# A fused attention and gated feed-forward kernel: how its last chunk is summed, transposed and stored, and where a small product of denominators stands

## The chip, the cores and the metric

The kernel runs on one core of a Trainium2 chip. The time is device microseconds of one execution. The five runs before the change gave 297.88, 298.35, 299.22, 299.48 and 301.63 us; their median is 299.22 us. A profile was taken of one further execution, and its trace has a time for every instruction of every engine.

## The reference

Everything is fp32.

```python
# attention: q, k, v are (4 batches, 4 heads, 1088 positions, 32)
a = einsum('rd,bhsd->bhsr', S1, x);  b = einsum('rd,bhsd->bhsr', S2, x)   # r = 8
phi(x) = (a outer b), 64 features
kv  = einsum('bhsf,bhsd->bhfd', phi(k), v);   z = sum(phi(k), axis=2)
num = einsum('bhsf,bhfd->bhsd', phi(q), kv)
den = einsum('bhsf,bhf->bhs', phi(q), z)[..., None] + 1e-06
x   = (num / den), laid out as (4352 tokens, 128)
# feed-forward: w_gate, w_val (128, 1536), w_out (1536, 128)
out = (1 / (1 + exp(-(x @ w_gate))) * (x @ w_val)) @ w_out
```

## The kernel before

The tokens of all four batches stand in one SBUF tensor `xT`, model dimension on partitions. Within a batch its columns are ordered so that 32 successive columns are 32 tokens that lie 34 apart in the output. The feed-forward part goes over `tok_chk`: chunks 0 to 7 of 512 tokens and chunk 8 of 256.

For a chunk, `w1` (lines 456 to 521) makes one wave at a time: the gate and value products of 128 hidden units for 512 tokens (in chunk 8: of 256 hidden units for 256 tokens, so six waves instead of twelve). ScalarE takes the sigmoid (line 479), VectorE the product `g` (line 501, run one slot later by `glu`). Then `g` is multiplied with `w_out`, in one of two ways:

- Chunks 1 to 7 use seven products in place of eight (`w2_a` and `w2_b`, matmuls at line 338, called `prod`), with sums of `g` made on GpSimd. When the last product of a chunk has been issued, five pieces of VectorE work are left: three steps of sums (line 410), a 64-partition transpose (line 445), and a second transpose followed by the chunk's stores. They are put into the list `moe["late"]`, and `slot` takes one of them per wave.
- Chunks 0 and 8 use `w2` (lines 362 to 386, matmuls at line 373, called `moeout`): `w_out` is stationary, `g` moves, and the result has the output features on partitions. A VectorE transpose (line 383) turns it in 32 x 32 blocks, and `store` writes it in four DMAs of one 32-feature group each, in runs of 32 numbers (128 bytes). For chunk 8 two of the four go out on ScalarE's queue, the others on SyncE's (SP). Chunks that cross a batch have eight.

In the trace one fp32 matmul of the program appears as two matmul instructions, each with a weight load. A matmul of 64 output rows uses half of the array's columns; two of them that write different halves run side by side.

The order of work is written by hand. `slot(group, waves)` first runs a piece of the attention part, then for each wave: `glu`, one item of `late`, every item of `todo` that has come due, and the next `w1`. `todo` holds the `w_out` products, with lags of 2 to 4 waves behind their `g`; when there are no more waves, the rest is issued one after the other. So chunk 7's five late pieces fall into the waves of chunk 8.

For the batches 1 to 3, `parts(b)` (line 1174) makes a batch's output of the attention. `den_j` (lines 930 to 943) multiplies into the PSUM tile `two`, and VectorE makes `pd` of it. `dn(b, n)` (line 972) issues the numerators of one half of the batch (`nps`, line 1000): n = 1 into the PSUM tile `wave`, n = 0 into the tile `two`, which is free again when `pd` has been made. `den_i` (line 946) multiplies `pd` with a mask into the spare columns of the `wave` tile (`nps`, line 949). `turn_den` transposes that and takes reciprocals on VectorE (line 961 on), and `divide1` and `divide0` write the quotients into `xT`.

PSUM tiles come from pools: `psm` has two buffers of the tile `wave`, `ps2` one of the tile `two`, each two banks wide. An instruction waits for semaphores of other engines; TensorE, VectorE and ScalarE each take their instructions in the order in which they were issued.

Of the kernel before, what the change touches and what calls it, by code (L numbers as in the profile page):

```python
# [8 lines left out]
F32 = mybir.dt.float32  # L9
# [7 lines left out]
P = 128  # L17
# [3 lines left out]
def kernel(  # L21
# [12 lines left out]
    nc = tc.nc  # L34

    B, H, S, D = q.shape
    R = S1.shape[0]
    F = R * R
    NTOK, DM = out.shape
    DFF = moe_w_gate.shape[1]  # L40
    NJ = DFF // P
    assert DM == H * D == P and D == 32 and R == 8 and S % 32 == 0

    T = S // 32

# [3 lines left out]
    TCH = 512  # L49
    tok_chk = [(o, min(TCH, NTOK - o)) for o in range(0, NTOK, TCH)]  # L50
# [3 lines left out]
    sbA = ctx.enter_context(tc.tile_pool(name="sbA", bufs=2))  # L54
# [7 lines left out]
    pso = ctx.enter_context(tc.tile_pool(name="pso", bufs=1, space=bass.MemoryType.PSUM))  # L62
    ps2 = ctx.enter_context(tc.tile_pool(name="ps2", bufs=1, space=bass.MemoryType.PSUM))
# [81 lines left out]
    w_sb = const.tile([P, 3, NJ, P], F32, tag="w_sb", name="w_sb")  # L145
# [133 lines left out]
    for c in range(2):  # L279
        rows = slice(64 * c, 64 * c + 64)  # L280
        nc.vector.tensor_reduce(
            out=m_col[rows, c],
            in_=ident[rows].rearrange("p (k j) -> p j k", j=R),
# [3 lines left out]
    for t, x in (  # L287
# [5 lines left out]
        out=e_sum,  # L293
        in_=bass.AP(
            tensor=e_row.tensor,
            offset=e_row.offset,
            ap=[list(e_row.ap[0]), [0, 2], [1, R], [0, R]],
        ),
# [43 lines left out]
    def store(ci, rows):  # L342
        t0, tw = tok_chk[ci]
        c = t0
        while c < t0 + tw:
            b, r = divmod(c, S)
            n = min(t0 + tw - c, S - r) // 32
            u = (c - t0) // 32
            for g4 in range(4):

                eng = nc.scalar if ci == len(tok_chk) - 1 and g4 % 2 else nc.sync
                eng.dma_start(
                    out=bass.AP(
                        tensor=out.tensor,
                        offset=out.offset + (b * S + r // 32) * DM + 32 * g4,
                        ap=[[T * DM, 32], [DM, n], [1, 32]],
                    ),
                    in_=rows(g4)[:, u : u + n, :],
                )
            c += n * 32  # L360

    def w2(ci, j0, jn, g):
        t0, tw = tok_chk[ci]
        if j0 == 0:
            moe["sum"] = ci
            if ci == 0:
                moe["acc"] = pso.tile([P, TCH], F32, tag="acc0", name="moeout")
            else:
                moe["acc"] = ps2.tile([P, 2, TCH], F32, tag="two", name="moeout")[:, 0]
        for jj in range(jn):  # L370
            j = j0 + jj
            for d in (slice(0, P),) if ci == 0 else (slice(0, 64), slice(64, P)):
                nc.tensor.matmul(  # L373
                    out=moe["acc"][d, :tw],
                    lhsT=w_sb[:, 2, j, d],
                    rhs=g[:, jj, :tw],
                    start=(j == 0),
                    stop=(j == NJ - 1),
                )
        if j0 + jn == NJ:  # L380
            o_sb = sbA.tile([P, 2, TCH // 32, 32], F32, tag="o_sb", name="o_sb")[:, 0]
            nt = tw // 32
            nc.vector.transpose(
                out=o_sb[:, :nt, :].rearrange("p t d -> p (t d)"), in_=moe["acc"][:, :tw]
            )
            store(ci, lambda g4: o_sb[32 * g4 : 32 * g4 + 32])


    fst = {}
# [66 lines left out]
    def w1():  # L456

        ci = moe["ci"]
        t0, tw = tok_chk[ci]
        jn = TCH // tw  # L460
        j0 = moe["w"] * jn
        wv = psm.tile([P, 2, TCH], F32, tag="wave", name="wave")

        tp = tw // 2 if ci == 0 and j0 == 0 else tw
        turn = (moe["w"] // 2) % 2
        for o in range(0, tw, tp):
            for which in range(2):
                for jj in range(jn):
                    for c in (0,) if ci == 0 else (1 - turn, turn):
                        d = slice(0, P) if ci == 0 else slice(64 * c, 64 * c + 64)  # L470
                        nc.tensor.matmul(  # L471
                            out=wv[d, which, jj * tw + o : jj * tw + o + tp],
                            lhsT=w_sb[:, which, j0 + jj, d],
                            rhs=xT[:, t0 + o : t0 + o + tp],
                            start=True,
                            stop=True,
                        )
        sg = sbG.tile([P, TCH], F32, tag="sg", name="sg")
        nc.scalar.activation(out=sg, in_=wv[:, 0], func=ACTF.Sigmoid)  # L479
        if ci == 0:  # L480
            if j0 == 1:
                narrow_01(2, 3)
            if 0 < j0 < NJ - 2:
                narrow_w(j0 + 1, 3)
            narrow_w(j0 + 2, 1)
            narrow_w(j0 + 2, 2)
            if j0 < 3:
                narrow_w(j0 + 3, 0)
            if j0 > 1:
                narrow_w(j0 + 4, 0)  # L490
            if j0 == NJ - 3:
                weight_sums(0, NJ // 4)
        if ci == 1 and j0 == 1:
            weight_sums(NJ // 4, NJ // 2)
        if moe["w"] % 2 == 0:
            moe["g"] = sbG.tile([P, 2, TCH], F32, tag="g", name="g")
        pair, odd, n = moe["g"], moe["w"] % 2, moe["n"]

        def glu():
            g = pair[:, odd]  # L500
            nc.vector.tensor_tensor(out=g, in0=wv[:, 1], in1=sg, op=MUL)  # L501
            todo = moe["todo"]
            if not fast(ci):
                lag = 3 if ci else 2
                part = (ci, j0, jn, g.rearrange("p (j t) -> p j t", j=jn))
                todo.append((n + lag, lambda: w2(*part)))
                return
            if not odd:
                moe["t"] = raw.tile([P, 4, HALF], F32, tag="w_in", name="tsum")
            token_sums(pair, moe["t"], odd)  # L510
            if odd:
                part = (ci, j0 // 2, pair, moe["t"])
                todo.append((n + 3, lambda: w2_a(*part)))
                todo.append((n + 4, lambda: w2_b(*part)))

        moe["gate"] = glu
        moe["w"] += 1
        moe["n"] += 1
        if j0 + jn == NJ:
            moe["ci"] += 1  # L520
            moe["w"] = 0
# [6 lines left out]
    def slot(group, waves):  # L528

        if group is not None:  # L530
            group()
        todo = moe["todo"]
        for _ in range(waves):
            more = moe["ci"] < len(tok_chk)
            if more and sum(tok_chk[moe["ci"]]) > moe["ready"]:
                break
            glu()
            if moe["late"]:
                moe["late"].pop(0)()
            while todo and todo[0][0] <= moe["n"]:  # L540
                todo.pop(0)[1]()
            if more:
                w1()
            elif not todo:
                break
            else:
                todo.pop(0)[1]()
# [398 lines left out]
    def den_i(b, t):  # L946
        dps = t[:, 0, W1 : W1 + WD]
        for h in range(H):
            nc.tensor.matmul(
                out=dps[32 * h : 32 * h + 32],  # L950
                lhsT=mask["head"][:, h % 2, :],
                rhs=PD[b][:, h // 2, :],
                start=True,
                stop=True,
            )
        return dps

    def turn_den(b, dps):
        nt, over = WD // 32, (W1 - WD) // 32
        dT = sbA.tile([P, nt, 32], F32, tag="dTi", name="dTi", bufs=1)  # L960
        nc.vector.transpose(out=dT.rearrange("p t c -> p (t c)"), in_=dps)
        RC[b] = sbA.tile([P, 2, W1 // 32, 2], F32, tag="rci", name="rci")
        for t0, t1, u0, k in ((0, nt, 0, 0), (nt, W1 // 32, nt - over, 4)):
            nc.vector.tensor_scalar_add(
                RC[b][:, :, t0:t1],
                dT[:, u0 : u0 + t1 - t0, k : k + 4].rearrange("p t (n c) -> p n t c", n=2),
                1e-6,
            )
        nc.vector.reciprocal(out=RC[b], in_=RC[b])
# [88 lines left out]
    else:  # L1058
        nc.vector.tensor_copy(
            out=s4[:, 1:],  # L1060
# [8 lines left out]
        out=st_[:, : 2 * R],  # L1069
        lhsT=s4.rearrange("p g d -> p (g d)"),  # L1070
# [103 lines left out]
    def parts(b):  # L1174
        den_j(b)
        glu()
        t = psm.tile([P, 2, 512], F32, tag="wave", name="nps")
        divide1 = dn(b, 1, t=t)
        divide0 = dn(b, 0)
        dps = den_i(b, t)  # L1180
        turn_den(b, dps)
        divide1()
        divide0()

# [101 lines left out]
```

## Time and profile before

| | us |
|---|---|
| median of five runs | 299.22 |
| lowest and highest run | 297.88, 301.63 |
| the profiled execution's own time | 301.79 |
| its span, from the first to the last instruction | 300.0 |
| TensorE busy with matmuls | 289.6 |
| VectorE busy | 187.1 |
| GpSimd busy | 161.4 |
| ScalarE busy | 88.8 |

The profile is of one core. PE stands for TensorE's matmuls and PEld for its weight loads, DVE for VectorE, ACT for ScalarE, POOL for GpSimd, SP for SyncE; SPq and ACTq are the queues on which SP and ScalarE issue DMAs. L373 is line 373 of the kernel. A row of the timeline gives the start, the duration (of all that it merges), the engine, the line, the operation, output and input with partitions x elements, the count, and in brackets the idle time before it with what ended it. A row of the waits gives the waiting instruction, what it waited for, the sum in us and how often. Matmul records overlap, since matmuls are pipelined.

### The profile page before, as it was taken

To read this page: it belongs to the slowest core of one execution; us is meant where nothing else is said; L and a number is where in the kernel's file an instruction comes from. 1 tells how busy PE (TensorE), PEld (TensorE's weight loads), DVE (VectorE), ACT (ScalarE), POOL (GpSimd) and SP (SyncE) were. 2 spreads that over 40 slices of the span, in tenths; PEclk is the share of its full clock that TensorE was granted. 3 is DMA by queue.
4 is the path that set the end of the run, shared out by engine and by line. 5 is a ranking of instruction groups with operands and counts; after the bars stand their busy time and mean duration, and the time that the engine had idled before them with its cause. 6 is when DMAs were issued, how large, how long until landed. Compare 5 with 4: busy or idle time off the path is not lost.

```text
span 300.0 us, 5678 instructions
## 1 busy us (share of the span) xinstructions
PE 289.6 (97%) x2224; PEld 154.9 (52%) x2224; DVE 187.1 (62%) x317; ACT 88.8 (30%) x164; POOL 161.4 (54%) x221
## 2 busy tenths in 40 slices
PE   8899999997999999999999999999999999999993
PEld 3444432353455456554455555554565655555892
DVE  6997789974725766677656695667436423643353
ACT  3556523222023222331223222422232222322320
POOL 2465553992364657645456498554455555565200
PEclk9999999999799999999999999999999999999998
DMA  7994340774700058426000475102000200020003
GB/s 225 356 327 101 101 139 13 163 154 103 237 0 0 11 132 165 129 76 177 9 0 2 124 176 111 26 0 37 1 2 0 35 2 0 0 37 0 2 0 52
DMA packets 29689, 24.21 MB, mean 81 GB/s; under 512 B 19616, under 2 KB 24864, under 8 KB 29664
## 3 DMA queue, kind: packets, MB, share of 16 engines
q1 hardware_dynamic: 28752, 23.10, 30.3%
q10 hardware_dynamic: 912, 0.77, 1.0%
q8 instruction: 17, 0.28, 0.4%
q14 instruction: 8, 0.07, 0.1%
HBM read 20.60 MB, written 3.26 MB: 80 GB/s over the span
## 4 chain that ended last, share of the span: by engine, by line
PE 76%; DMA 13%; DVE 4%; POOL 2%; SPq 2%; issue 1%; ACT 1%; POOLq 0%; ACTq 0%
PE wave L471 49%; PE prod L338 20%; DMA bq<-dq 5%; PE moeout L373 3%; DMA w_in<-in_moe_w_out_dram 2%; POOL head L118 2%; DMA w_in<-in_moe_w_gate_dram 2%; DMA v<-in_v_dram 2%; DVE w_sb L127 1%; PE nps L1000 1%; DMA kq<-in_k_dram 1%; DVE head L109 1%; SPq L758 1%; DMA dq<-cq 1%; PE kvz L806 1%
## 5 line engine op out<-in xcount | busy, mean ns | idle before, releaser
L471 PE MATMUL wave<-xT,w_sb 128*64 128x512 f32 (+3 forms) x820 | 211.5, 566 | 0.1
L501 DVE TENSOR_TENSOR g<-wave,sg 128x512 f32<-128x512 f32 x102 | 70.0, 687 | 86.8 <-ACT sg L479 85.4
L471 PEld LDWEIGHTS wave<-xT,w_sb 128*64 128x64 f32 (+1 forms) x820 | 85.5, 140 | 64.7 <-issue 49.3
L479 ACT ACTIVATE sg<-wave 128x512 f32<-128x512 f32 x102 | 61.0, 598 | 184.3 <-PE wave L471 183.1
L328 POOL TENSOR_TENSOR tsum<-g 128x256 f32<-128x256 f32 x84 | 68.0, 812 | 26.1 <-DVE g L501 25.9
L328 POOL TENSOR_TENSOR tsum<-g,tsum 128x256 f32<-128x256 f32 x42 | 34.2, 814 | 66.6 <-DVE g L501 66.1
L338 PE MATMUL prod<-tsum,ws 128*64 128x256 f32 x252 | 64.2, 384 | 0.0
L338 PEld LDWEIGHTS prod<-tsum,ws 128*64 128x64 f32 x252 | 31.8, 138 | 15.8 <-issue 10.9
L338 PE MATMUL prod<-g,w_sb 128*64 128x256 f32 x168 | 34.8, 382 | 0.0
L328 POOL TENSOR_TENSOR tsum<-tsum,g 128x256 f32<-128x256 f32 x42 | 32.8, 780 | 3.3
L338 PE MATMUL prod<-tsum,w_sb 128*64 128x256 f32 x84 | 25.9, 390 | 0.0
L338 PEld LDWEIGHTS prod<-g,w_sb 128*64 128x64 f32 x168 | 15.9, 136 | 17.7 <-issue 15.3
L338 PE MATMUL prod<-g,ws 128*64 128x256 f32 x84 | 25.0, 379 | 0.0
L118 POOL TENSOR_TENSOR head<-head,tail 128x384 int32<-128x384 int32 (+2 forms) x14 | 13.4, 954 | 18.2 <-DVE head L109 12.9
L373 PE MATMUL moeout<-g,w_sb 128*64 128x256 f32 (+1 forms) x72 | 18.7, 456 | 0.3 <-DVE w_sb L127 0.3
L338 PEld LDWEIGHTS prod<-g,ws 128*64 128x64 f32 x84 | 11.5, 137 | 3.3
L338 PEld LDWEIGHTS prod<-tsum,w_sb 128*64 128x64 f32 x84 | 10.9, 138 | 4.5 <-issue 4.0
L786 DVE TENSOR_TENSOR qp<-qp,bq 128x1152 f32<-128x1152 f32 (+1 forms) x7 | 9.6, 1374 | 5.1 <-DMA bq<-dq 3.7
L373 PEld LDWEIGHTS moeout<-g,w_sb 128*64 128x64 f32 (+1 forms) x72 | 8.8, 154 | 7.0 <-issue 2.8
L666 DVE TENSOR_TENSOR kp<-kab 128x1152 f32<-128x1152 f32 (+2 forms) x10 | 10.7, 1082 | 0.0
L445 DVE STREAM_TRANSPOSE o_sb<-res 64x512 f32<-64x512 f32 x14 | 9.6, 688 | 0.0
L410 DVE TENSOR_TENSOR res<-prod,other 64x512 f32<-64x512 f32 (+1 forms) x14 | 7.6, 544 | 2.8 <-ACT other L404 2.8
(111 smaller groups left out, 185.1 us busy)
## 6 DMA issues: line engine op xcount, KB each, us to landing
qp<-dq SPq DMA_DIRECT2D x7, 576.0 KB, 10.4
bq<-dq SPq DMA_DIRECT2D x14, 288.0 KB
kq<-in_k_dram SPq DMA_DIRECT2D x3, 544.0 KB, 4.1
kq<-in_q_dram SPq DMA_DIRECT2D x3, 544.0 KB
w_in<-in_moe_w_out_dram SPq DMA_DIRECT2D x6, 256.0 KB
w_in<-in_moe_w_gate_dram SPq DMA_DIRECT2D x5, 256.0 KB
w_in<-in_moe_w_val_dram SPq DMA_DIRECT2D x5, 256.0 KB, 6.4
out_dram<-o_sb SPq DMA_DIRECT2D x20, 64.0 KB, 2.3
```

The source lines that it names most:

```text
L109: nc.vector.scalar_tensor_tensor(out=head, in0=cap, scalar=-0x40000000, in1=head, op0=ALU.bitwise_and, op1=ALU.bitwise_or)
L118: nc.gpsimd.tensor_tensor(out=head, in0=head, in1=tail, op=ALU.add)
L328: nc.gpsimd.tensor_tensor(out=t[:, u], in0=in0, in1=in1, op=ALU.subtract)
L338: nc.tensor.matmul(out=out, lhsT=lhsT, rhs=rhs, start=start, stop=stop, skip_group_check=True)
L373: nc.tensor.matmul(out=moe["acc"][d, :tw], lhsT=w_sb[:, 2, j, d], rhs=g[:, jj, :tw], start=(j == 0), stop=(j == NJ - 1),)
L410: nc.vector.tensor_tensor(out=out, in0=in0, in1=in1, op=op)
L445: nc.vector.transpose(out=o_sb[:64, d].rearrange("p t x -> p (t x)"), in_=r[:, 1 + 2 * d : 3 + 2 * d].rearrange("p u x -> p (u x)"),)
L471: nc.tensor.matmul(out=wv[d, which, jj * tw + o : jj * tw + o + tp], lhsT=w_sb[:, which, j0 + jj, d], rhs=xT[:, t0 + o : t0 + o + tp], sta ...
L479: nc.scalar.activation(out=sg, in_=wv[:, 0], func=ACTF.Sigmoid)
L501: nc.vector.tensor_tensor(out=g, in0=wv[:, 1], in1=sg, op=MUL)
L666: eng.tensor_tensor(out=KP[b][:, pi, j0:j1].rearrange("p j m (i l) -> p (j m) i l", i=R), in0=bass.AP(tensor=a0.tensor, offset=a0.offset, ...
L786: nc.vector.tensor_tensor(out=q0, in0=q0, in1=half(BQ[b], n), op=MUL)
```

## The change

Three edits:

1. While the waves of chunk 8 run, `slot` takes two items of `late` per wave instead of one.
2. Chunk 8's `w_out` products are done by a new function, `w2_end`: `g` is stationary, 64 tokens at a time, and `w_out` moves with 128 columns. The result has tokens on partitions, so there is no transpose. The 256 tokens are two halves `u` of 128, each in a PSUM bank of the tile `two`. Half 0 is copied to SBUF by ScalarE and stored by SP, half 1 copied by VectorE and stored by ScalarE's queue, each in one DMA of runs of 128 numbers (512 bytes). `w2` keeps chunk 0 alone.
3. In `parts`, `den_i` and `turn_den` stand between the numerators of n = 1 and those of n = 0, instead of behind both.

```diff
+    def store_end(o_sb, u):
+        b, r = divmod(tok_chk[-1][0] + u * P, S)
+        (nc.scalar if u else nc.sync).dma_start(
+            out=bass.AP(
+                tensor=out.tensor,
+                offset=out.offset + (b * S + r // 32) * DM,
+                ap=[[DM, P // 32], [T * DM, 32], [1, DM]],
+            ),
+            in_=o_sb[:, u],
+        )
...
+    def w2_end(ci, j0, jn, g):
+        if j0 == 0:
+            moe["sum"] = ci
+            moe["acc"] = ps2.tile([P, 2, TCH], F32, tag="two", name="moeout")
+        acc = moe["acc"]
+        if j0 + jn == NJ:
+            o_sb = sbA.tile([P, 2, P], F32, tag="o_sb", name="o_end")
+        for u in range(2):
+            for jj in range(jn):
+                j = j0 + jj
+                for c in (u * P, u * P + 64):
+                    nc.tensor.matmul(
+                        out=acc[c % P : c % P + 64, u, :DM],
+                        lhsT=g[:, jj, c : c + 64],
+                        rhs=w_sb[:, 2, j, :],
+                        start=(j == 0),
+                        stop=(j == NJ - 1),
+                    )
+            if j0 + jn == NJ:
+                (nc.scalar.copy if u == 0 else nc.vector.tensor_copy)(
+                    out=o_sb[:, u], in_=acc[:, u, :DM]
+                )
+                store_end(o_sb, u)
...
-                todo.append((n + lag, lambda: w2(*part)))
+                todo.append((n + lag, lambda: (w2_end if ci else w2)(*part)))
...
-            if moe["late"]:
-                moe["late"].pop(0)()
+            for _ in range(2 if moe["ci"] >= len(tok_chk) - 1 else 1):
+                if moe["late"]:
+                    moe["late"].pop(0)()
...
         divide1 = dn(b, 1, t=t)
+        turn_den(b, den_i(b, t))
         divide0 = dn(b, 0)
-        dps = den_i(b, t)
-        turn_den(b, dps)
         divide1()
         divide0()
```

More of the change, by code (lines that the diff above doesn't have):

```diff
@@ L41 @@
     NJ = DFF // P
-    assert DM == H * D == P and D == 32 and R == 8 and S % 32 == 0
+    assert DM == H * D == P and D == 32 and R == 8 and S % 32 == 0 and NTOK % 512 == 256
     T = S // 32
@@ L349, in store @@
             for g4 in range(4):
-                eng = nc.scalar if ci == len(tok_chk) - 1 and g4 % 2 else nc.sync
-                eng.dma_start(
+                nc.sync.dma_start(
                     out=bass.AP(
@@ L360, in store @@
             c += n * 32
+    def store_end(o_sb, u):
[8 more added lines that the diff above has]
+        )
     def w2(ci, j0, jn, g):
-        t0, tw = tok_chk[ci]
         if j0 == 0:
             moe["sum"] = ci
[L366 to L369, printed above, removed]
+            moe["acc"] = pso.tile([P, TCH], F32, tag="acc0", name="moeout")
@@ L370, in w2 @@
         for jj in range(jn):
             j = j0 + jj
[L372 to L379, printed above, removed]
+            nc.tensor.matmul(
+                out=moe["acc"],
+                lhsT=w_sb[:, 2, j, :],
+                rhs=g[:, jj],
+                start=(j == 0),
+                stop=(j == NJ - 1),
+            )
@@ L380, in w2 @@
         if j0 + jn == NJ:
             o_sb = sbA.tile([P, 2, TCH // 32, 32], F32, tag="o_sb", name="o_sb")[:, 0]
[L382 to L385, printed above, removed]
+            nc.vector.transpose(out=o_sb.rearrange("p t d -> p (t d)"), in_=moe["acc"])
             store(ci, lambda g4: o_sb[32 * g4 : 32 * g4 + 32])
+    def w2_end(ci, j0, jn, g):
[9 more added lines that the diff above has]
+                for c in (u * P, u * P + 64):
+                    nc.tensor.matmul(
+                        out=acc[c % P : c % P + 64, u, :DM],
+                        lhsT=g[:, jj, c : c + 64],
+                        rhs=w_sb[:, 2, j, :],
+                        start=(j == 0),
+                        stop=(j == NJ - 1),
+                    )
+            if j0 + jn == NJ:
+                (nc.scalar.copy if u == 0 else nc.vector.tensor_copy)(
+                    out=o_sb[:, u], in_=acc[:, u, :DM]
+                )
+                store_end(o_sb, u)
```

## The prediction

> **What bounds the kernel now.** I read the page's busy times first, then the chain that ended last over the final 10 us, then VectorE and the two DMA queues over the same stretch, then the waits.
>
> ```profile
> span 300.0 us, 5678 instructions
> PE 289.6 (97%) x2224; PEld 154.9 (52%) x2224; DVE 187.1 (62%) x317; ACT 88.8 (30%) x164; POOL 161.4 (54%) x221
> ```
>
> TensorE is busy for 97% of the span. In the matmul records from 15 us on, the only gaps over 0.1 us are those round the denominators of each batch and one of 0.33 us at 18.8. So between 15 and 292 us a change pays only if it takes work from TensorE or closes such a gap. The end is another stage:
>
> ```profile
> 290.83 1.73 PE wave L471 x16
> 292.56 2.60 PE moeout L373 x24
> 295.16 0.02 issue
> 295.18 0.45 DVE o_sb L383
> ```
>
> TensorE ends at 295.14, VectorE turns the last result at 295.18, and 4.4 us of the span are left with nothing but stores. The timeline shows what they do:
>
> ```profile
> 290.72 0.69 DVE L501 TENSOR_TENSOR g<-wave,sg 128x512 f32<-128x512 f32 x1 [1.06 <-ACT sg L479]
> 291.33 0.40 DVE L410 TENSOR_TENSOR res<-res,other 64x256 f32<-64x256 f32 x1
> 291.77 0.68 DVE L410 TENSOR_TENSOR res<-res 64x512 f32<-64x512 f32 x1
> 293.24 0.69 DVE L501 TENSOR_TENSOR g<-wave,sg 128x512 f32<-128x512 f32 x1 [0.79 <-ACT sg L479]
> 293.85 1.28 DVE L445 STREAM_TRANSPOSE o_sb<-res 64x512 f32<-64x512 f32 x2
> 294.57 2.99 SPq L352 DMA_DIRECT2D out_dram<-o_sb  x6
> 295.67 0.91 ACTq L352 DMA_DIRECT2D out_dram<-o_sb  x2
> ```
>
> Of the six SP issues, four are chunk 7's stores; its last turn waits behind the last g. Their issues stand at 294.57, 294.93, 295.51 and 296.01, so the last chunk's two SP stores, whose data is ready at 295.63, go out at 296.62 and 297.11. The trace's landing events put the last of them at 299.06; barrier and drain take 0.94 us more to 300.0. ScalarE's two stores (295.67, 296.07) landed by 298.53. So chunk 7's late turn sets the end by 0.5 us over ScalarE's stores, and its traffic slows those too.
>
> **Part 1: two sums a slot.** The same five sums and turns, one slot earlier from the third on. VectorE after the g at 288.04: the two seventh/fifth sums end at 289.66 as now, then 0.40 + 0.68 us of last sums follow at once, to about 290.74; the g at 290.72 loses 0.02 us. After that g (to 291.41) come both turns, 1.28 us, to 292.7, before the last g at 293.24: still hidden. TensorE's next use of these g lies one to three slots later, so nothing waits. On SP, chunk 7's four stores, about 0.5 us each, move to 292.1-294.8: that queue is free at 294.8. Price 0 on TensorE (0.02 us if the cover goes). If only this were done, SP would issue the last chunk's two at 295.67 and 296.07 like ScalarE, 1.0 us earlier than now. That is its worth: about 1.0 us of the end.
>
> **Part 2: the last chunk with g stationary.** Before: 24 matmuls, each two instructions in the trace, of 256 moving columns. After: 48 of 128 columns. Columns are the same, instructions and weight loads double from 48 to 96. Now a set of 8 instructions on two column halves takes 0.86 us, 0.216 us per pair. The nearest row for the new form:
>
> ```profile
> L871 PEld LDWEIGHTS ndps<-ident,kvd x12: 137/137/137, 66.7 to 186.7; 128*64 128x64 f32 x12
> L871 PE MATMUL ndps<-ident,kvd x12: 272/273/273, 67.1 to 186.8; 128*64 128x128 f32 x12
> ```
>
> (shortest, median and longest in ns): the same 64-wide tile with 128 moving columns. Its pairs start 0.109 us apart in all three batches (67.095, 67.204, then the next product at 67.313), though each has its own load. The kvz matmuls (32-wide, 64 columns) even run four loads per 0.056 us. The Trainium skill speaks against the change (TensorE: Matmul & The Clock Gate, "Back-to-back issue gap"): in a sustained stream of load and matmul, 128 columns cost about 81 ns a matmul against 56 isolated, because loads come in. By that rule the six sets (5.2 us) would grow by 45%, 2.3 us, all on TensorE's path; by the row they grow by 0.01 us each. I take the row, since it is this tile with fresh weights each time; the rule stays as the upper end. Below nothing I exclude: the columns are the same.
>
> The last set then begins at 294.1 (now 294.06; its g is ready at 293.93). Token half 0: four pairs, 3 x 0.11 + 0.06 + 0.27 = 0.66, to 294.76. ScalarE's copy out of PSUM waits for it: the 128x128 nd copy (L879) took 0.26 us, with 0.05 before it: 295.07. In the built program the first matmul of token half 1 waits for that copy (both halves are one PSUM tile), though its bank is another. This wait is new; behind it on TensorE stand the last four matmuls, and VectorE's copy and the last store wait for them. So TensorE restarts at 295.12 and ends at 295.12 + 0.05 + 0.33 + 0.27 = 295.77 instead of 295.14. VectorE's copy (no copy of this size out of PSUM is in the trace; 0.22 by the 128x128 copy L292 from SBUF, 0.32 carried down from the 128x160 and 128x256 turns at 0.349 and 0.451; I take 0.25) ends at 296.06, and ScalarE's queue issues the last store at 296.09. Half 0's store leaves SP at 295.12, which is free by then.
>
> How long a store takes to land decides the rest. Now stores are 32 x n runs of 128 B. One with n = 4 landed in 1.40 us, one with n = 16 in 1.79: 24 more packets an engine cost 0.39 us, 16 ns each (12 ns by the packet records), upon a base of 1.27. New: 128 runs of 512 B. The trace has 12 ns for 128 B and 47 for 1,024; between them 512 B is about 27, with the same 4 ns of spacing 31. Over 16 engines that is 8 x 31 = 0.25: landing 1.52. But the new store's outer dimension is 4 (4 x 32 x 128). The Trainium skill (DMA: Bandwidth & Descriptors, "Why a DMA increments its semaphore by 16 and not by 1") says a DMA runs on the largest number of engines up to 16 that divides the outer dimension of both sides. The trace agrees: a store with outer 32 raises its semaphore 16 times when data lands; a bq load with an outer 8 once, at 1.0 us, and eight times at landing. So I take 4 engines: 32 x 31 = 0.99, landing 2.26; the ends are 1.5 (16 engines) and 2.75 (45 ns a packet).
>
> Last landing 296.09 + 2.26 = 298.35, against 299.06. SP's closing waits have one step more after this semaphore, 0.06. Saved: 0.65 us, say 0.7. Part 2 thus gives back some 0.35 of part 1's gain: the wait on ScalarE and the four engines eat what fewer, longer packets save.
>
> **Part 3: denominators between the numerators.** The order on TensorE was den_j, numerators n=1, numerators n=0, den_i; now den_i stands before n=0, three times (waits: us in total, times, longest):
>
> ```profile
> DVE dTi L961 <- PE nps L949: 2.5, 3, 1.3
> PEld nps L1000 <- DVE pd L943: 2.1, 3, 0.7
> ```
>
> TensorE's wait for pd (the gaps of 0.13 to 0.17 us in its matmul records) is met by den_i instead of the n=0 numerators, at the same moment, since pd also frees the bank that they write. A matmul of another tile shape starts 0.09 us late (numerators to den_i at 140.94, den_i to prod at 141.35): two such changes before and two after, the third lying inside the gap. VectorE's turn starts about 0.6 us sooner (140.9 for 141.49), at the earliest after its g at 140.89. Who gains? Nobody on the path: no gap of TensorE between the batches is ended by these divisions. A new wait of the n=0 numerators names TensorE's own den_j, finished long before. So 0, with 0.3 us either way (one shape change more, or less, per batch).
>
> **Sum.** The profiled execution's own time is 301.79, span 300.0 and 1.8 around it; less 0.7 gives 301.1. That execution is 2.6 over the median of 299.22: its clock stood at 0.59 from 75.3 to 79.5 us, after a wait for the b load,
>
> ```profile
> 75.30:79.50 4.20, 4.07 (x55) 1.66 (x57) 2.34 (x8) 0.00 (x0) 2.83 (x4) 0.59 0.91 241
> ```
>
> 3.4 us at half speed, 1.7 us lost, and the runs range over 3.75 us. The change touches nothing ahead of that wait, so I take the saving off the median: 298.5 us.
>
> **Rivals.**
> *A, the forecast:* the end 0.4 to 1.0 us earlier, 298.2 to 298.8. Chance 0.5.
> *B, the stores land as fast as on 16 engines:* 0.74 us less, 297.8; for it, 512 B packets and an empty queue; against it, the eight-engine bq load. Chance 0.2.
> *C, slower: weight loads bound the 128-column form.* At the skill's rate +2.3 us, net 1.6 slower, 300.8. For it: loads double to 96 and each lasts 0.137 us, longer than 0.109. Against: ndps and kvz. It decides once a pair takes more than 0.109 + 0.7/48 = 0.124 us. Chance 0.1.
> *D, it doesn't do what it says:* the ScalarE wait and four slow engines (2.75 us) eat all of part 1: 299.2. Chance 0.2.
>
> About 1% (3 us) is what a measurement of this kernel can tell from no change; none of these reaches it, so only scatter of the half-speed stretch could. Faster by over 1%: 0.03; within: 0.91; slower: 0.06. The range, 297.2 to 300.4, holds A, B and D with about 0.8 of median scatter, and most of C.
>
> **What would show it.** In the profile after: the turns of chunk 7 at 291.4-292.7 and SP's four stores from 292.1; TensorE ending near 295.8 with an idle of 0.3 to 0.4 us before its last eight instructions, released by ScalarE's copy; moeout pairs 0.11 us apart (0.14 or more is C); the last store issued by ScalarE near 296.1, its semaphore rising four times; 1.0 us after it the end. The prediction is wrong if moeout's sets of 16 take over 1.0 us, if the last landing is not the ScalarE store, or if a batch's den_i opens a gap over 0.3 us.

## The result and the profile after

The changed kernel took 297.94 us (median of 36 runs, 296.50 to 299.94); the kernel before, run beside it and earlier, 299.03 us (median of 71, 297.58 to 303.42). The ratio is 0.9963, with a 95% interval of 0.9950 to 0.9975: 1.10 us faster, between 0.75 and 1.5. Here and below a ratio leaves out the few runs over 1.5% above the fastest of their kernel, and it is not just the quotient of the two medians. The forecast was 298.5, 0.7 us faster. The total is near by luck: two of its terms were wrong, with opposite signs.

The profiled execution of the changed kernel took 297.61 us, with a span of 295.8. Its span cannot be set against the 300.0 of before: that execution had the wait for the b load and the half-speed stretch behind it that the prediction tells of, and this one has neither. The page of the changed kernel begins:

```profile
span 295.8 us, 5780 instructions
PE 288.4 (97%) x2272; PEld 155.2 (52%) x2272; DVE 186.7 (63%) x317; ACT 89.0 (30%) x165; POOL 161.4 (55%) x221
```

There are 48 matmuls and 48 weight loads more than before, and TensorE is still busy for 97%. To compare places I use lengths between two instructions that both kernels have. *The ending* is the time from the first matmul of the last wave to the end of the span. A store *lands* with the last rise of its semaphore in the trace; "landed 2.5 us later" counts from its issue. The last wave before:

```profile
290.61 1.95 PE L471 MATMUL wave<-xT,w_sb 128*64 128x256 f32 x16
```

The ending was 9.40 us before (from 290.61) and is 9.13 after (from 286.68). That is 0.27 us, a quarter of what was gained. The timeline of the ending after (start, duration, engine and line; in brackets the engine's idle time before it and what ended it):

```profile
286.68 1.95 PE L496 MATMUL wave<-xT,w_sb 128*64 128x256 f32 x16
286.78 0.69 DVE L526 TENSOR_TENSOR g<-wave,sg 128x512 f32<-128x512 f32 x1
287.39 1.29 DVE L470 STREAM_TRANSPOSE o_sb<-res 64x512 f32<-64x512 f32 x2
288.11 1.96 SPq L350 DMA_DIRECT2D out_dram<-o_sb  x4
288.41 2.40 PE L400 MATMUL moeout<-w_sb,g 128*64 128x128 f32 x40
289.31 0.69 DVE L526 TENSOR_TENSOR g<-wave,sg 128x512 f32<-128x512 f32 x1 [0.64 <-ACT sg L504]
290.85 0.27 ACT L408 COPY o_end<-moeout 128x128 f32<-128x128 f32 x1 [1.57 <-DMA out_dram<-o_sb]
291.14 0.60 SPq L362 DMA_DIRECT2D out_dram<-o_end  x1
291.17 0.66 PE L400 MATMUL moeout<-w_sb,g 128*64 128x128 f32 x8 [0.35 <-ACT o_end L408]
291.93 0.29 DVE L408 COPY o_end<-moeout 128x128 f32<-128x128 f32 x1 [1.92 <-PE moeout L400]
292.25 1.12 ACTq L362 DMA_DIRECT2D out_dram<-o_end  x1
```

What was foretold of the order is there: chunk 7's turns stand ahead of the last g, SP is done with chunk 7 before it gets half 0's store at 291.14, TensorE stands idle for 0.35 us before its last eight instructions, released by ScalarE's copy, and ScalarE's queue issues the last store, 5.57 us after the wave began. (The copy's row names a DMA, but it starts 0.04 us after the end of TensorE's 40 instructions, as it does in the run of part 2 alone, where the row names TensorE.)

### The profile page after: what moved, and what is told of

The parts are those of the page before. It is cut to its first block, busy times and chain, and to the rows that moved or that the text cites. A ratio compares the mean times of both kernels' runs of the same rounds, so it can differ in the third digit from the quotient of the medians.

```text
span 295.8 us, 5780 instructions
## 1 busy us (share of the span) xinstructions
PE 288.4 (97%) x2272; PEld 155.2 (52%) x2272; DVE 186.7 (63%) x317; ACT 89.0 (30%) x165; POOL 161.4 (55%) x221
## 3 DMA queue, kind: packets, MB, share of 16 engines
HBM read 20.60 MB, written 3.26 MB: 81 GB/s over the span
## 4 chain that ended last, share of the span: by engine, by line
PE 81%; DMA 8%; DVE 5%; POOL 2%; issue 1%; SPq 1%; ACT 1%; POOLq 0%; DVEq 0%; ACTq 0%
PE wave L496 53%; PE prod L338 22%; DMA v<-in_v_dram 3%; DMA w_in<-in_moe_w_out_dram 2%; POOL head L118 2%; DMA w_in<-in_moe_w_gate_dram 2%; PE moeout L377 1%; PE kvz L832 1%; DVE w_sb L127 1%; DVE head L109 1%; PE nps L1026 1%; DVE head L105 1%; DVE res L435 1%; DMA out_dram<-o_sb 1%; PE denj L961 1%
## 5 line engine op out<-in xcount | busy, mean ns | idle before, releaser
L328 POOL TENSOR_TENSOR tsum<-g 128x256 f32<-128x256 f32 x84 | 67.0, 800 | 23.7 <-DVE g L526 23.5
L338 PE MATMUL prod<-tsum,ws 128*64 128x256 f32 x252 | 62.3, 381 | 0.0
L338 PEld LDWEIGHTS prod<-tsum,ws 128*64 128x64 f32 x252 | 30.9, 137 | 16.7 <-issue 12.6
L328 POOL TENSOR_TENSOR tsum<-tsum,g 128x256 f32<-128x256 f32 x42 | 33.6, 801 | 3.3
L377 PE MATMUL moeout<-g,w_sb 128*128 128x512 f32 x24 | 12.7, 610 | 0.3 <-DVE w_sb L127 0.3
L260 PE MATMUL warm<-const-float32-1.0 128*128 128x512 f32 (+1 forms) x12 | 7.6, 767 | 0.8 <-PEq L1295 0.8
```

Of the source, the lines that this page charges most:

```text
L260: nc.tensor.matmul(out=t[:, 0, :n], lhsT=x, rhs=r, start=True, stop=True)
L328: nc.gpsimd.tensor_tensor(out=t[:, u], in0=in0, in1=in1, op=ALU.subtract)
L338: nc.tensor.matmul(out=out, lhsT=lhsT, rhs=rhs, start=start, stop=stop, skip_group_check=True)
L377: nc.tensor.matmul(out=moe["acc"], lhsT=w_sb[:, 2, j, :], rhs=g[:, jj], start=(j == 0), stop=(j == NJ - 1),)
```

## The experiments

Each kernel is told by its edit. Times are medians; each ratio is to the kernel before, run beside it on the same chip.

| kernel | median, us | before, us | ratio (95%) | ending, us | den_i of batch 2 to that of batch 3, us |
|---|---|---|---|---|---|
| changed | 297.94 | 299.03 | 0.9963 (0.9950 to 0.9975) | 9.13 | 64.78 |
| part 1 alone | 297.80 | 298.97 | 0.9957 (0.9940 to 0.9974) | 8.22 | 65.18 |
| part 2 alone | 299.95 | 298.97 | 1.0032 (1.0018 to 1.0045) | 10.06 | 65.18 |
| part 3 alone | 298.05 | 298.97 | 0.9973 (0.9957 to 0.9989) | 9.38 | 64.78 |
| parts 1 and 3, old ending | 296.78 | 298.97 | 0.9928 (0.9909 to 0.9948) | 8.22 | 64.78 |
| changed, late turn | 298.95 | 298.95 | 0.9991 (0.9971 to 1.0010) | 9.11 | 65.18 |
| changed, one copy | 298.19 | 298.95 | 0.9978 (0.9956 to 1.0000) | 9.59 | 64.79 |
| changed, outer dimension 32 | 297.78 | 298.95 | 0.9962 (0.9939 to 0.9985) | 8.90 | 64.79 |
| changed, both of these | 297.28 | 298.95 | 0.9937 (0.9915 to 0.9959) | 8.66 | 64.78 |

The last column is a difference of two starts, 206.12 - 140.94 in the kernel before and 201.96 - 137.18 in the changed one (first the rows of before, then of after):

```profile
140.94 0.48 PE L949 MATMUL nps<-pd,head 128*32 128x160 f32 x8
206.12 0.48 PE L949 MATMUL nps<-pd,head 128*32 128x160 f32 x8
```

```profile
137.18 0.48 PE L975 MATMUL nps<-pd,head 128*32 128x160 f32 x8 [0.17 <-DVE pd L969]
201.96 0.48 PE L975 MATMUL nps<-pd,head 128*32 128x160 f32 x8 [0.17 <-DVE pd L969]
```

It runs from one den_i to the next, so it takes in what follows the denominators of batch 2 and leaves the ending out.

### Each part by itself

Part 1 alone, on the kernel before:

```diff
-            if moe["late"]:
-                moe["late"].pop(0)()
+            for _ in range(2 if moe["ci"] >= len(tok_chk) - 1 else 1):
+                if moe["late"]:
+                    moe["late"].pop(0)()
```

> Part 1 alone (two sums a slot) on the kernel before. The tail is counted from the first matmul of the last wave to the end of the span: 9.40 us before, 9.13 after. Theory (SP's queue held back the last chunk's stores): SP issues them at once when the turn ends, the last landing comes 1.0 us sooner, tail 8.4, time 0.997 of before. Rival (the landing is bound by the DMA engines, not by the queue): tail 9.2 to 9.4. In both the batches' second wave behind the denominators still starts 0.86 us after the products before it.

The ending went from 9.40 to 8.22 us, 1.18 less (1.0 was forecast). Its timeline:

```profile
288.45 1.28 DVE L445 STREAM_TRANSPOSE o_sb<-res 64x512 f32<-64x512 f32 x2
289.17 4.42 SPq L352 DMA_DIRECT2D out_dram<-o_sb  x6
292.31 0.45 DVE L383 STREAM_TRANSPOSE o_sb<-moeout 128x256 f32<-128x256 f32 x1 [1.25 <-PE moeout L373]
292.79 0.89 ACTq L352 DMA_DIRECT2D out_dram<-o_sb  x2
```

Chunk 7's turns lie before the last g. (In the kernel before, VectorE stood idle for 0.79 us ahead of that g although the turn's input had been ready since 292.45: the turn stood behind the g in VectorE's order.) Of SP's six issues the last two now stand beside ScalarE's (5.05 and 5.41 us after the wave, ScalarE's 5.06 and 5.48; in before SP's last two stood at 6.01 and 6.50). The last landing is at 7.31. So the last issue came forward by 1.02, and the landing behind it by a little more.

Part 2 alone, on the kernel before (`store_end` and `w2_end` as in the diff shown above the prediction):

```diff
-                todo.append((n + lag, lambda: w2(*part)))
+                todo.append((n + lag, lambda: (w2_end if ci else w2)(*part)))
```

> Part 2 alone (g stationary in the last chunk). Theory: SP still issues chunk 7's four stores from about 4.0 us after the last wave's start, but only one store of the last chunk is behind them; TensorE ends 0.6 us later by the wait on ScalarE's copy, the four-engine stores land after 2.5 us: tail 9.1 to 9.5, so 0 to 0.3 us off before, ratio 0.999 to 1.001. Rival (part 2 is what gained): tail 8.5 or less.

```profile
292.22 1.94 SPq L350 DMA_DIRECT2D out_dram<-o_sb  x4
293.84 1.12 ACTq L362 DMA_DIRECT2D out_dram<-o_end  x1
294.26 0.60 SPq L362 DMA_DIRECT2D out_dram<-o_end  x1
```

It is slower than before, by 0.5 to 1.35 us, and its ending grew by 0.66, to over 0.5 more than expected. Here chunk 7's turns still stand behind the last g, so that SP reaches half 0's store only after chunk 7's four, 6.00 us after the wave (which began at 288.26), later than ScalarE's at 5.57. It landed 3.16 us after that, where 2.5 was expected; ScalarE's store was still under way. On top of part 1 the same edit costs 9.13 - 8.22 = 0.91 us. The forecast had 0.35.

Part 3 alone, on the kernel before:

```diff
         divide1 = dn(b, 1, t=t)
+        turn_den(b, den_i(b, t))
         divide0 = dn(b, 0)
-        dps = den_i(b, t)
-        turn_den(b, dps)
```

> Part 3 alone (den_i between the numerators). Theory now: the gain sits here. Before, the second wave behind a batch's denominators waited for the wave tile that the first division frees (0.43 us in batches 2 and 3); den_i earlier lets the division end before TensorE asks: the wave starts 0.44 us after the products before it instead of 0.86, 0.9 to 1.3 us over the kernel, tail unchanged at 9.4, ratio 0.9955 to 0.997. Rival, the prediction's step (nobody waits for the divisions): no change, ratio 1.000.

It is faster than before, by 0.3 to 1.3 us, and it was forecast at zero. The ending hardly moves (9.38). From den_i of batch 2 to that of batch 3 TensorE needs 0.40 us less; from batch 1 to batch 2 0.24 less (62.62, against 62.86 with part 1 alone and 62.90 with part 2 alone; the half-speed stretch of the kernel before lies there). From batch 3 to the last wave it needs 0.20 more, but den_i itself now stands 0.60 sooner, so it is 0.40 less there too. That is 1.04 us in all.

Parts 1 and 3 with the ending of before:

```diff
-                todo.append((n + lag, lambda: (w2_end if ci else w2)(*part)))
+                todo.append((n + lag, lambda: w2(*part)))
```

(with `w2` and `store` as in the kernel before).

> Parts 1 and 3 without part 2. Theory: tail as with part 1 alone (8.4), 0.9 to 1.3 us less in the batches: 2.0 us under before, about 0.9 us under the changed kernel, ratio 0.993. Rival (part 2 is needed for the gain at the end): tail 9.1 or more, ratio 0.996 or above.

296.78 us, 2.2 under the kernel before, and faster than the changed kernel, too: the upper end of its interval, 0.9948, lies below the lower end of the changed kernel's, 0.9950. The parts add up: 1.18 of the ending and 1.04 of the batches are 2.22, measured 2.15 (1.55 to 2.7). Part 2 then takes 0.91 back: 1.31, measured 1.10 (0.75 to 1.5).

### Where part 3's microsecond comes from

The prediction looked for idle time of TensorE between matmul records and found none that these divisions end. The timeline of the kernel before, behind the denominators of batch 2, shows why it missed the one that is there:

```profile
141.49 0.35 DVE L961 STREAM_TRANSPOSE dTi<-nps 128x160 f32<-128x160 f32 x1 [0.60 <-PE nps L949]
143.94 0.76 DVE L1025 TENSOR_TENSOR xT<-nps,rb 128x576 f32<-128x576 f32 x1
143.98 0.38 PE L338 MATMUL prod<-tsum,ws 128*64 128x256 f32 x1
144.41 0.59 PE L338 MATMUL prod<-tsum,ws 128*64 128x256 f32 x2
144.81 0.23 PEld L471 LDWEIGHTS wave<-xT,w_sb 128*64 128x64 f32 x4 [0.26 <-issue]
144.84 1.08 PE L471 MATMUL wave<-xT,w_sb 128*64 128x512 f32 x4
```

Until then two products run side by side, one on each half of the array's columns (the first two start 0.006 us apart, at 143.98). From 144.41 only one half has work: two products run on it one after the other, to 145.0, while the wave that should take the other half starts at 144.84. A PSUM tile of the tag `wave` holds the numerators and denominators of the batch, and the second wave behind them takes its place; the last to read it is VectorE's product (L1025), which ends at 144.70. The wave waits for VectorE's semaphore, which rises at that moment in the trace, and its weight load follows 0.11 us later. The row calls the wait "issue", and the matmul of the other half covers it, so it is not among the gaps between matmul records.

In the changed kernel the same stretch, from the timeline:

```profile
137.72 0.35 DVE L987 STREAM_TRANSPOSE dTi<-nps 128x160 f32<-128x160 f32 x1
139.96 0.76 DVE L1051 TENSOR_TENSOR xT<-nps,rb 128x576 f32<-128x576 f32 x1
140.81 0.38 PE L338 MATMUL prod<-tsum,ws 128*64 128x256 f32 x1
141.25 0.59 PE L496 MATMUL wave<-xT,w_sb 128*64 128x512 f32 x1
141.25 0.57 PEld L496 LDWEIGHTS wave<-xT,w_sb 128*64 128x64 f32 x4
```

The turn of the denominators starts 3.09 us before the second group of products (140.81 - 137.72), where it was 2.49 (143.98 - 141.49): 0.60 us sooner. The product ends at 140.72, before that group begins, and the wave starts 0.44 us behind it on the free half instead of 0.86. The difference, 0.42, is the 0.40 of the table.

To test this, the changed kernel got its division back late: VectorE turns the same denominators three times over, with the same output, and TensorE's order stays the new one.

```diff
         nc.vector.transpose(out=dT.rearrange("p t c -> p (t c)"), in_=dps)
+        for _ in range(2):
+            nc.vector.transpose(out=dT.rearrange("p t c -> p (t c)"), in_=dps)
```

> The changed kernel with the transposition of the denominators done three times over on VectorE (the two repeats add some 0.6 us to that chain, TensorE's order stays). Theory (part 3 gains because the division frees the wave tile earlier): the second wave behind the denominators waits again; all its matmuls start 0.8 us or more after the products before it instead of 0.44, about 0.4 us a batch in batches 2 and 3, so den_i to den_i of batches 2 and 3 goes from 64.78 back to about 65.2; 1.0 us over the kernel, ratio about 0.9995 of before. Rival (TensorE's order of shapes gains by itself): 64.78 stays, ratio 0.996.

```profile
143.91 0.76 DVE L1053 TENSOR_TENSOR xT<-nps,rb 128x576 f32<-128x576 f32 x1
144.38 0.59 PE L338 MATMUL prod<-tsum,ws 128*64 128x256 f32 x2
144.78 0.23 PEld L496 LDWEIGHTS wave<-xT,w_sb 128*64 128x64 f32 x4 [0.26 <-issue]
144.81 0.65 PE L496 MATMUL wave<-xT,w_sb 128*64 128x512 f32 x2
```

The timeline shows the picture of before again: the product ends at 144.67, the wave starts 0.86 us behind the products, and 65.18 us lie between den_i of batches 2 and 3, with TensorE's new order untouched. By the lengths, 0.85 of the changed kernel's 1.31 us are taken back (0.40 twice, and 0.05 in batch 1); the ratio, 0.9991, has an interval from 0.87 us faster to 0.3 slower, which holds the 0.46 that should be left. So in batches 2 and 3 the order on TensorE by itself is worth nothing, and VectorE's earlier start is worth all of it.

In batch 1 the tile is taken by a later wave and the wait is shorter. With part 1 alone its weight load stands at 78.89, 0.12 us behind the product's end at 78.77; that is 3.28 us behind the first products after the denominators (75.61). With part 3 the product ends sooner and the wave follows at 3.07, which is most of the 0.24 us measured there. The late turn ends the product at 2.97 instead of 3.16, so the wave stands at 3.12 and brings 0.05 of the 0.24 back (62.67 us between the two den_i), not all of it.

### What part 2 costs, and whether it can be had cheaper

Two causes were named for the 0.91 us: ScalarE's copy, for which TensorE waits, and the stores on four engines. One experiment takes each away, and one both.

First the wait. All matmuls come before the copy, and VectorE copies both halves in one instruction:

```diff
-            if j0 + jn == NJ:
-                (nc.scalar.copy if u == 0 else nc.vector.tensor_copy)(
-                    out=o_sb[:, u], in_=acc[:, u, :DM]
-                )
+        if j0 + jn == NJ:
+            nc.vector.tensor_copy(out=o_sb, in_=acc[:, :, :DM])
+            for u in range(2):
                 store_end(o_sb, u)
```

> The changed kernel with both token halves' matmuls first, then one VectorE copy of 128x256, then the two stores (still four engines each). Theory: TensorE's wait on ScalarE's copy is gone (its last matmul ends 4.55 to 4.65 us after the last wave's start instead of 5.14), the copy takes about 0.42, both stores are issued at 5.05 to 5.15 instead of 5.57 and share four engines, so the last lands 2.5 to 3.3 us later: tail 8.5 to 9.2 (9.13 in the changed kernel). Rival (the wait is the whole price of part 2): tail 8.2.

TensorE ends 4.57 us after the wave began instead of 5.14, and both stores are issued at 5.06 instead of the last at 5.57. Yet the ending is 9.59, longer than the changed kernel's and than the 8.5 to 9.2 expected. The rows of the copied tile (duration in ns, shortest, median, longest):

```profile
L362 SPq DMA_DIRECT2D out_dram<-o_end x1: 602/602/602, 295.1 to 295.1; - x1
L362 ACTq DMA_DIRECT2D out_dram<-o_end x1: 1429/1429/1429, 295.1 to 295.1; - x1
```

Issued together, the two stores landed 2.75 and 3.49 us later, against 2.53 for the changed kernel's last, which was issued 1.1 us behind the other. In the packet records ScalarE's store sends its first packet 2.08 us after its issue, where it took 1.28 in the changed kernel, and while packets of both are under way, 4.0 of them move at a time, as many as of one such store alone. The two share four engines. Taking the wait away brings the issue 0.5 us forward, and running both stores at once takes 0.96 away again.

Second the engines. The last chunk's g is written with its columns in another order, so that the store's outer dimension is 32 instead of 4:

```diff
-                ap=[[DM, P // 32], [T * DM, 32], [1, DM]],
+                ap=[[T * DM, 32], [DM, P // 32], [1, DM]],
...
-            nc.vector.tensor_tensor(out=g, in0=wv[:, 1], in1=sg, op=MUL)
+            x = [g, wv[:, 1], sg]
+            if ci == len(tok_chk) - 1:
+                x = [g.rearrange("p (a s t) -> p a t s", s=32, t=4)] + [
+                    y.rearrange("p (a t s) -> p a t s", s=32, t=4) for y in x[1:]
+                ]
+            nc.vector.tensor_tensor(out=x[0], in0=x[1], in1=x[2], op=MUL)
```

> The changed kernel with the last chunk's g written in another column order, so that a store's outer dimension is 32 instead of 4. Theory (the outer dimension sets the number of engines): 16 landing events instead of 4, and the last store lands 1.4 to 1.7 us after its issue instead of 2.53: tail 8.1 to 8.4 (9.13 in the changed kernel). Rival (long because it is the last, or because of ScalarE's queue): landing stays at 2.4 us or more, tail 9.0 or more.

```profile
289.33 1.10 DVE L531 TENSOR_TENSOR g<-wave,sg 128x512 f32<-128x512 f32 x1
```

```profile
L362 ACTq DMA_DIRECT2D out_dram<-o_end x1: 627/627/627, 292.6 to 292.6; - x1
DMA to landing us min/median/max: 2.0/2.0/2.0
```

(First the timeline, then the rows of the copied tile.) The semaphore of each store now rises sixteen times at landing, and the last lands 1.98 us after its issue instead of 2.53: that is what four engines cost, 0.55 (the store's packets take 0.36 us instead of 0.92). But it is not the 1.4 to 1.7 expected, and the strided write takes 1.10 us instead of 0.69, on the path: the last matmuls end 5.46 us after the wave instead of 5.14. The ending is 8.90, only 0.23 better than the changed kernel. (SP's four issues of chunk 7 took 3.26 us here and 1.96 in the changed kernel, so half 0's store left 0.58 us after its copy; why is open. It landed before the other half's and does not set this ending.)

With both edits at once:

> The changed kernel with both: one copy behind both halves, and stores of outer dimension 32. Theory: last matmul ends at 4.6, copy to 5.05, issues at 5.1, landing 1.5 to 1.7 later, tail 7.5 to 7.8: 0.5 us better than part 1 with the old ending (8.22), 1.4 us better than the changed kernel, ratio about 0.991 of before. Rival (the two costs overlap and one alone decides): tail 8.2 or more.

The issues stand at 5.38, the landings 2.00 and 2.25 us later, and the ending is 8.66, not the 7.5 to 7.8 expected: the last matmul ends at 4.88 instead of 4.6, behind the strided write, and the landings were put at 1.5 to 1.7. The median, 297.28, is under the changed kernel's, but this ending is still 0.44 us longer than the 8.22 of the old one behind part 1. Even without the wait and with all engines, g stationary did not pay here: its stores need 2.0 to 2.25 us to land, and the many short ones that they replace 1.83 from the last issue on (7.31 - 5.48). A cheaper way to the outer dimension of 32, which leaves the write of g as it was, was not tried; the 0.3 us that the last matmuls would gain (4.57 for 4.88) would, by this sum, leave the ending near 8.35, an estimate.

## Why the prediction was right, and where it was wrong

- **Part 1: right in place, near in size.** 1.0 forecast, 1.18 measured. The turns moved as foretold, 0.71 to 2.00 us after the wave, and the g of 286.78 was not held up. One sum was off without harm: four stores of about 0.5 us from 292.1 on free SP's queue at 294.1, not at 294.8; measured, they took 1.96 us.
- **TensorE's work in part 2: right.** The pairs of the new form start 0.109 us apart (288.410, 288.519, 288.628), and a slot with a set of 16 in it lasts 2.60 us from wave to wave (284.08 to 286.68) as it did before with 2.59. A set of 16 is eight such pairs, 0.87 us from start to start, under the 1.0 that would have shown the prediction wrong. The row of `ndps` was the right one to go by; the 81 ns rule in the Trainium skill (TensorE: Matmul & The Clock Gate, "Back-to-back issue gap"), and with it rival C, is not seen in these sets. Taken at its word it would have cost 2.3 us, by estimate.
- **Part 2's wait: right.** 0.35 us idle (0.36 by the forecast's 294.76 to 295.12), ScalarE's copy 0.27 for 0.26, VectorE's copy 0.29 for 0.25, the last issue at 5.57 where the working gives 296.09 - 290.61 = 5.48.
- **Part 2's landing: right in mechanism, wrong in size.** Four engines were taken, as the Trainium skill says (DMA: Bandwidth & Descriptors, "Why a DMA increments its semaphore by 16 and not by 1"). The trace agrees: the last store's semaphore rises once at 1.2 us and four times at 2.44 to 2.53, and 4.0 of its packets move at a time on average (9.5 with the outer dimension of 32). But the landing was put at 2.26 and is 2.53; on sixteen engines it is 1.98, where 1.52 was worked out. A packet of 512 B took 27 ns, as estimated, and all of them 0.92 us (0.99 was worked out) and 0.36 (0.25). The mis-sized term is the base, 1.27 us from SP's stores of 128 B runs: what the packets leave over is 1.61 on four engines and 1.63 on sixteen. Of that, 1.28 pass from the issue to the first packet, where chunk 7's first store needs 0.84. (The slow end of 2.75 is 2.71 by the forecast's own numbers, 1.27 + 32 x 0.045.) So part 2 gives back 0.91 and not 0.35: 0.27 more of landing, 0.09 of a later issue, and 0.18 because the old ending was better behind part 1 than forecast (1.18 for 1.0); 0.02 are left over.
- **Part 3: the step that failed.** "Nobody on the path: no gap of TensorE between the batches is ended by these divisions." That is wrong: the path does gain. In each batch one column half of TensorE waited for the PSUM tile that these divisions free, 0.24 us longer in batch 1 and 0.40 in batches 2 and 3 than with the new order; it was hidden by looking for gaps in the records of all matmuls together, where one busy half of the array covers the other. It is worth 1.04 us, well beyond the 0.3 that was allowed. TensorE's wait for `pd` was read rightly: den_i now meets it, with 0.17 us at most, and no gap over 0.3 opened.
- **The rivals.** The median, 297.94, lies near B's number, 297.8, but not by B's mechanism: the stores did run on four engines. D's mechanism, the wait and the slow stores eating what part 1 brings, is most of what the ending shows (0.27 us left of 1.18), and the total is nonetheless near A because part 3 brought what no rival held. That is luck: 0.27 and 1.04 were measured where 0.7 and 0 were forecast.

## What to carry to other kernels

Where work is laid on two column halves of TensorE, look for idle time in each half by itself, and ask of each PSUM tile who reads it last and which matmul takes its place; a wait of 0.4 us a batch can stand under 97% busy, labelled "issue". A late result of an engine that is far from busy can still hold the bound engine through the buffer it has not yet given back. And before many short stores are replaced by few long ones, compare the time from the last issue to the last landing, not packets or instructions: here the short ones, spread over sixteen engines and two queues, were done sooner.

## What had not been expected of the hardware

- A store of 128 runs of 512 B, 64 KB, lands 1.98 us after its issue on 16 engines and 2.53 on four. One of 512 runs of 128 B, the same 64 KB, landed in 1.79. Longer runs alone bought nothing.
- Issuing such a store from ScalarE's queue takes 1.12 us on four engines (in part 2 alone too, where SP's was issued after it) and 1.43 beside one issued at the same time, against 0.63 on sixteen; SP's takes 0.60 to 0.64 in all of them.
- Two four-engine stores issued together landed at 2.75 and 3.49 us: 4.0 packets of both move at a time where they overlap, so they share the same engines.
- VectorE's product out of PSUM into SBUF took 1.10 us where it wrote every fourth number in turn (steps of 16 bytes) and 0.69 with columns in order, for the same 128x512.
